# A new order for the steps behind the first sentence's weight transfers

## The chip, the cores and the metric

The kernel runs on one core of a Trainium2 chip. The metric is the device time of one execution in microseconds (us), taken as the median of several runs; lower is better.

## The reference

Eight sentences of 576 tokens go through causal sliding-window attention (window 64, 8 heads of 64), and each sentence then goes whole to one of eight experts, which is picked from the mean of its attention output.

```python
scores = np.where(mask, scale * np.matmul(q, k.transpose(0, 1, 3, 2)), -1e9)   # mask: 0 <= i - j < 64
attn = np.exp(scores - scores.max(-1)); attn /= attn.sum(-1) + 1e-09
x = np.matmul(attn, v)                       # then heads side by side: (8, 576, 512)
logits = x.mean(axis=1) @ w_gate             # (8 sentences, 8 experts)
e_idx, gate_w = argmax(logits), softmax(logits)[e_idx]
out[b] = gate_w[b] * (np.maximum(x[b] @ w1[e_idx[b]], 0) @ w2[e_idx[b]])   # F = 1024
```

## The kernel before

Nothing loops over the work in the usual sense. The table `OPS` at the top of the file lists 890 steps; one loop walks it and calls a small function for each step, with the scheduler set to keep the order as written. So the place of a step in the table is the place of its instructions in the queue of each engine that it uses. An engine takes its instructions strictly in this order; between engines there are only semaphores.

A step is a letter, sometimes letters for an engine or a buffer (`a` ACT, `d` DVE, `m` the shared PSUM pool, `b` a mask added by TensorE), and a number. Units are counted through: unit 5b+i is head pair i of sentence b for i below 4 (512 tokens), and the last 64 tokens of all heads for i = 4.

- Transfers, all on GpSimd's queue: `Q` loads q or k of a sentence (512 KB), `t` the q and k of its last 64 tokens (two transfers of 64 KB, L133), `L` a fifth of its v (128 KB, the last one 64 KB; L141, L145), `W` a half of w1 or w2 of its expert (512 KB; L423, L426; `W4b` and `W4b+1` are w1, `W4b+2` and `W4b+3` are w2), `O` a store of 128 tokens by GpSimd (`o` by SP). `P` reads the picked expert into a register of GpSimd.
- Attention: `T` transposes q and k on TensorE (L225), `U` and `k` copy them out of PSUM, `S` makes scores (L275), `E` the exponential on ACT (L288), `K` the mask product on DVE (L297), `l` the row sums on TensorE (L309), `n` and `R` the logarithm and the reciprocal on ACT (L351, L357), `A` the product with v (L331), `X` the division on DVE (L364). `V` copies v of a sentence once more on DVE, moved by 64 rows (L150, L151); `A` of a sentence needs it.
- Gate of a sentence: `g`, `j`, `G`, `H`, `I`.
- Expert: each `c` is the next chunk of matmuls, for each sentence nine of w1 (L461, the ninth L470) and then nine of w2 (four blocks in two halves of 8 matmuls, L503; the second half is the first to read the second half of w2; then L512). Each `r` empties the PSUM buffer of the oldest finished chunk, on ACT or on DVE (L446, L448, L482, L487).

The chunks share a pool of three PSUM buffers with those `T`, `S` and `A` that carry an `m`; a chunk waits until the buffer used three allocations earlier has been emptied. GpSimd's transfers go round eight semaphores (named DMASW0 to DMASW7 below): a transfer is issued when the one eight places before it has landed.

```python
c, x = op[0], op[1:].lstrip("abdm")
e = op[1:len(op) - len(x)]
if c == "c":
    todo.pop(0)()
elif c in "oO":
    store(nc.sync if c == "o" else nc.gpsimd)
elif c == "r":
    evac.pop(0)(e)
```

Of the kernel before, what the change touches and what calls it, by code (L numbers as in the profile page):

```python
# [1 line left out]
OPS = (  # L2
    "Y0.24 Q0.48 Q1.48 Q0.2 Cd0.24 y i Q1.2 Y1.24 Q3 Cd1.24 z Tm3 Tm2 mb T0 Tm1 ka3 ka2 ka0 "
    "t0 Ud3 Ud2 Q2 Sb3 L0 L3 ka1 L1 L2 E3 Smb2 L4 Ud0 l3 Ud1 t1 S0 T4 E2 kd4 Ud4 n3 Smb1 E0 "
    "Mb K0 E1 R3 Q4 L9 Tm5 Sb4 Tm7 Tm8 Ud5 Q5 ka5 kd8 E4 L5 kd7 l1 n1 T6 l4 n4 Ud7 l2 Sb5 ka6 "
    "n2 R1 R4 l0 V0 A3 Ud6 L7 Am1 n0 E5 T9 X3 Am2 Ud9 S7 R2 L8 E7 Ud8 X1 R0 l5 X2 L6 n5 Smb6 "
    "A0 Am4 K7 ka9 E6 t2 X4 X0 Sb8 l7 g0 n7 T12 j0 Q6 Sm9 Tm10 G0 Ud12 kd12 E8 Ud10 H0 E9 "
    "Tm13 Tm11 R7 K9 l6 R5 ka10 Sb12 Ud11 ka13 V1 n6 Q7 l8 P0 Ud13 W0 I0 kd11 T14 Am5 A7 X7 "
    "A6 Ud14 kd14 L12 n8 X5 E12 R6 l12 n12 Sm14 X6 S11 l9 E14 Smb10 Tm17 E11 n9 T18 W1 Ud17 "
    "A9 W2 E10 S13 kd18 Ud18 L13 Tm15 Ud15 l10 Am8 R8 W3 kd15 ka17 T16 K14 L11 c X8 L14 n10 "  # L10
    "E13 R9 c ra X9 c R10 c rd c g1 K11 rd S17 j1 G1 ra ra c H1 L10 c rd l14 K13 c t3 ra c P1 "
    "n14 Q8 ra c c rd c V2 Ua16 c c ra ka16 l11 A10 X10 Am12 W4 c Q9 R12 X12 n11 ra W5 R11 "
    "A11 rd W6 T19 E17 c l13 n13 R13 Ua19 I1 X11 c Sm18 S15 K17 L15 rd E18 W7 R14 A13 c l17 "
    "ra X13 A14 c L16 L17 X14 g2 n17 Tm20 E15 ra kd19 c Ud20 ra L18 kd20 T22 S19 Sm16 E19 L19 "
    "j2 G2 c P2 t4 K15 E16 Q10 K18 c ra c W8 H2 ra ka22 c ra c c S20 l18 ra rd rd K16 c n18 "
    "Q11 K19 L21 ra Tm21 c c Ua21 Ud22 l16 W9 T23 R17 kd21 L23 V3 c c R18 c ra Am17 Ud23 n16 "
    "ra l15 E20 X17 L22 c R16 ka23 c rd n15 A18 c S23 X18 Sm21 K20 T24 kd24 ra R15 E21 L20 "
    "A16 c l19 L29 ra L24 W10 n19 Ud24 Am15 X16 A19 W11 R19 c X15 l20 E23 n20 L25 I2 c X19 rd "
    "L26 ra Tm26 c g3 K23 kd26 l23 Ud26 R20 c ra Sm22 n23 S24 j3 rd G3 E24 E22 T28 H3 K21 c "
    "Tm27 Ud28 P3 t5 ka27 kd28 l21 L28 rd n21 I3 K24 S26 L27 T25 c V4 W12 c Ua27 ra l24 c K22 "  # L20
    "c ra ra ra Ud25 n24 c R23 Q13 Q12 Am20 X20 R21 c c c rd Am23 W13 kd25 E26 A21 T29 rd X23 "
    "l22 Sm27 W14 W15 n22 E27 S28 V5 c c K26 K27 L32 c R24 l26 c X21 t6 A24 E28 Am22 ra R22 "
    "L30 ra K28 n26 X24 Ud29 kd29 c A27 l27 n27 c X22 ra ra c g4 S25 R26 rd Sm29 j4 G4 L34 "
    "E29 T32 Tm30 kd30 E25 Ud30 c Ua32 H4 K29 P4 ka32 ra c l28 R27 T33 L33 rd Ua33 S30 I4 n28 "
    "c Q15 c ra L31 ra Am26 ka33 c E30 c ra W16 X27 X26 ra l29 c K25 R28 c rd n29 Q14 A28 K30 "
    "c W17 X28 T34 S32 Sm33 ra O O E32 c E33 c K32 l25 n25 R25 c kd34 Am25 A29 W18 c O Ua34 "
    "R29 rd W19 T31 l30 c X29 X25 rd ka31 g5 c c Ud31 O ra K33 rd Sm31 n30 S34 j5 G5 c V6 R30 "
    "P5 rd O E31 H5 c K31 T36 l32 Ud36 rd E34 c t7 c A30 c n32 I5 rd L39 ka36 ra R32 l33 T35 "
    "X30 A32 Ua35 L38 rd c K34 rd c ka35 c n33 T37 ra Sm35 S36 L37 O E35 rd c X32 ra E36 W20 "
    "l34 c L35 n34 c K35 K36 L36 c kd37 R33 c O l31 rd W21 R34 rd c n31 R31 c Ua37 Tm38 O W23 "  # L30
    "Ud38 A33 ra ka38 Am34 l35 T39 X33 c n35 W22 c ra X34 A31 X31 g6 kd39 c O Sm38 R35 O S37 "
    "ra E38 j6 c c G6 P6 Ud39 E37 ra ra c V7 K38 rd H6 c l36 c K37 W24 n36 S39 A35 l37 ra rd "
    "E39 c ra n37 c X35 R36 c A37 c ra l38 Am36 K39 ra c c O R37 rd X37 n38 Am39 X36 O c rd c "
    "I6 l39 W27 R38 c n39 O O A38 rd R39 c W25 W26 ra X39 X38 g7 c j7 O c G7 c ra c P7 rd ra "
    "c c O W29 O c ra c O rd H7 O ra c O c W28 W31 ra O ra O c ra c c ra rd c c c c rd c W30 "
    "I7 O ra O c rd c c ra rd O c O O rd c O rd O O c rd c c O ra c c rd c O rd ra rd c c O "
    "rd O c c ra O O c c c c ra rd o O c ra O c ra o "
).split()

# [554 lines left out]
```

## Time and profile before

| | |
|---|---|
| runs | 204.0, 204.12 and 203.14 us, median 204.0 |
| span of the profiled execution, first to last instruction | 201.9 us |
| what the median has beyond that span | 2.1 us |
| granted TensorE clock | 0.996 |
| TensorE busy, DVE, ACT, GpSimd | 183.5, 119.9, 131.8, 111.0 us |
| moved by DMA | 41.16 MB, mean 204 GB/s |

No time of the profiled execution itself is given beside its span, so the span is what the working below starts from, and 2.1 us are carried over as they are. Rows of the profile have a line of the kernel, an engine, an operation, the tile written and those read; "idle before" is the time in which the engine stood still ahead of an instruction, and what ended it. In the chain of waits each row has start, length and the work.

### The profile page before, as it was taken

What the parts mean: (1) busy time and instruction counts of PE and PEld (TensorE: products, weight loads), DVE (VectorE), ACT (ScalarE), POOL (GpSimd) and SP (SyncE); (2) the same over time, 40 slices, a digit from 0 to 9 for tenths busy, and PEclk for the clock granted to TensorE, in tenths of its full rate; (3) what the DMA queues carried; (4) which work ended last, traced back from release to release, by engine and by line L of the source; (5) the groups of instructions that cost most, each with busy time, mean ns of one, the idle gap of its engine ahead of it and who ended that gap; (6) DMA issues with size and microseconds to landing.
All of it is one profiled execution on the core that took longest, in us unless ns stands there. A gap on an engine that the chain in (4) does not pass through costs nothing.

```text
span 201.9 us, 8105 instructions
## 1 busy us (share of the span) xinstructions
PE 183.5 (91%) x3518; PEld 124.2 (62%) x3522; DVE 119.9 (59%) x347; ACT 131.8 (65%) x247; POOL 111.0 (55%) x158
## 2 busy tenths in 40 slices
PE   0487886899999999999999999999999999999991
PEld 0455564656677756577667666676656666776760
DVE  3527989595477546895877457966494651216410
ACT  2179998876599578977779975757787436321121
POOL 7985939235931593478633552439452716553561
PEclk9999999999999999999999999999999999999998
DMA  6999999999999999999999999999999999999693
GB/s 135 175 188 159 194 162 198 199 198 174 196 201 197 170 198 193 174 201 167 200 206 200 169 195 223 259 208 137 183 237 243 266 254 212 274 212 301 235 325 134
DMA packets 83346, 41.16 MB, mean 204 GB/s; under 512 B 48080, under 2 KB 80976, under 8 KB 83312
## 3 DMA queue, kind: packets, MB, share of 16 engines
q0 software_dynamic: 81936, 39.72, 138.5%
q1 hardware_dynamic: 768, 0.85, 1.3%
q8 instruction: 27, 0.44, 0.8%
q10 hardware_dynamic: 608, 0.08, 0.2%
q14 instruction: 7, 0.06, 0.1%
HBM read 61.88 MB, written 9.44 MB: 353 GB/s over the span
## 4 chain that ended last, share of the span: by engine, by line
PE 77%; DMA 9%; POOL 7%; issue 3%; DVE 2%; ACT 1%; POOLq 0%; DVEq 0%; ACTq 0%
PE ph L461 28%; PE po L503 25%; DMA vw<-in_v_dram 9%; PE tp L225 5%; PE ph L470 4%; PE s L275 4%; PE av L331 3%; PE po L512 3%; PE lb L309 3%; POOL vw L141 2%; POOL km L110 2%; POOL qm L110 1%; POOL out_dram L492 1%; PE gps L392 1%; POOL qkt L133 1%
## 5 line engine op out<-in xcount | busy, mean ns | idle before, releaser
L503 PE MATMUL po<-w2b,hm 128*64 128x512 f16 x512 | 60.1, 379 | 0.0
L461 PE MATMUL ph<-xm,w1b 128*64 128x512 f16 x512 | 60.0, 379 | 0.0
L461 PEld LDWEIGHTS <-w1b 128*64 128x64 f16 x512 | 31.7, 110 | 18.7 <-issue 0.4
L503 PEld LDWEIGHTS <-hm 128*64 128x64 f16 x512 | 30.1, 110 | 19.3
L141 POOL DMA_DIRECT2D vw<-in_v_dram x32 | 28.9, 910 | 13.3 <-DMA w1b<-in_moe_w_dram 4.3
L446 ACT ACTIVATE hm<-ph,gw 128x512 f16<-128x512 f32 x39 | 26.6, 693 | 13.4 <-PE ph L461 13.3
L492 POOL DMA_DIRECT2D out_dram<-ob x31 | 17.2, 557 | 25.0 <-DMA w1b<-in_moe_w_dram 7.0
L351 ACT ACTIVATE ln<-lb 128x512 f32<-128x512 f32 (+1 forms) x40 | 22.5, 563 | 11.8 <-PE lb L309 8.6
L364 DVE CUSTOM_DVE_ANT_0 xm<-av,rl 128x512 f16<-128x512 f32 x32 | 21.6, 686 | 10.4 <-PE av L331 9.5
L482 ACT COPY ob<-po 128x512 f32<-128x512 f32 x18 | 10.6, 586 | 23.6 <-PE po L503 23.6
L448 DVE TENSOR_SCALAR hm<-ph,gw 128x512 f16<-128x512 f32 x25 | 18.7, 748 | 12.1 <-PE ph L461 11.6
L357 ACT ACTIVATE rl<-ln 128x512 f32<-128x512 f32 (+1 forms) x40 | 23.3, 594 | 1.5 <-DVE pool L364 1.3
L225 PE MATMUL tp<-ident,qm 128*64 128x128 bf16 x256 | 13.8, 232 | 7.4 <-DMA qm<-in_q_dram 6.9
L288 ACT ACTIVATE pe<-s 128x1024 f16<-128x1024 f32 x19 | 19.5, 1028 | 1.4 <-PE s L275 0.7
L297 DVE TENSOR_TENSOR pe<-pe,mask 128x1024 f16<-128x1024 f16 x24 | 16.3, 687 | 3.9 <-ACT pe L288 3.1
L252 ACT COPY kT<-tp 128x512 bf16<-128x512 bf16 x19 | 11.2, 597 | 9.0 <-PE tp L225 8.0
L225 PEld LDWEIGHTS <-qm 128*64 128x64 bf16 x256 | 10.7, 118 | 10.0 <-DMA qm<-in_q_dram 6.9
L482 DVE COPY ob<-po 128x512 f32<-128x512 f32 x14 | 9.7, 690 | 10.7 <-PE po L503 10.5
L423 POOL DMA_DIRECT2D w1b<-in_moe_w_dram x16 | 12.6, 785 | 5.9 <-DMA vw<-in_v_dram 2.9
L275 PEld LDWEIGHTS <-kT 64*128 64x128 bf16 x576 | 10.1, 95 | 8.9 <-issue 5.6
L331 PEld LDWEIGHTS <-vw 128*64 128x64 f16 x512 | 12.4, 112 | 4.7 <-issue 1.2
L225 PE MATMUL tp<-ident,km 128*64 128x128 bf16 x256 | 13.9, 231 | 1.4 <-DMA km<-in_k_dram 0.9
(80 smaller groups left out, 267.2 us busy)
## 6 DMA issues: line engine op xcount, KB each, us to landing
w1b<-in_moe_w_dram POOLq DMA_DIRECT2D x16, 512.0 KB, 9.3
w2b<-in_moe_w_dram POOLq DMA_DIRECT2D x16, 512.0 KB, 13.4
out_dram<-ob POOLq DMA_DIRECT2D x31, 256.0 KB, 8.1
vw<-in_v_dram POOLq DMA_DIRECT2D x32, 128.0 KB, 9.0
km<-in_k_dram POOLq DMA_DIRECT2D x7, 512.0 KB, 9.3
qm<-in_q_dram POOLq DMA_DIRECT2D x7, 512.0 KB, 9.0
out_dram<-obt POOLq DMA_DIRECT2D x14, 64.0 KB, 7.7
qkt<-in_q_dram POOLq DMA_DIRECT2D x8, 64.0 KB, 7.6
```

The lines of the kernel that those rows point to most:

```text
L141: nc.gpsimd.dma_start(out=vt[:, 2 * J + 1], in_=v[b, :, 128 * J:128 * J + 128].rearrange("h c d -> c h d"))
L225: nc.tensor.transpose(tp[p0:p0 + 64, n, r], t[:, 2 * i + hh, ts(r, 64)], ident)
L288: nc.scalar.activation(out=po, in_=sp[0], func=AF.Exp, scale=scale)
L351: nc.scalar.activation(out=ln, in_=lb[:, 0:n], func=AF.Ln)
L357: nc.scalar.activation(out=rl, in_=lns.pop((b, i)), func=AF.Exp, scale=-1.0)
L364: nc.vector.tensor_tensor_reduce(out=xm[:, i], in0=av.rearrange("q r p -> q (r p)"), in1=rl, scale=1.0, scalar=0.0, op0=ALU.mult, op1=ALU.add,
L446: nc.scalar.activation(out=o, in_=i, func=AF.Relu, scale=g)
L448: nc.vector.tensor_scalar(out=o, in0=i, scalar1=g, scalar2=0.0, op0=ALU.mult, op1=ALU.max)
L461: nc.tensor.matmul(out=ph[64 * c:64 * c + 64], lhsT=w1t[:, kb, ts(2 * ft + c, 64)], rhs=xm[:, kb], start=(kb == 0), stop=(kb == 3), skip_g ...
L482: copy(e)(out=ob, in_=po)
L492: (nc.scalar if n and eng is nc.sync else eng).dma_start(out=dst, in_=src)
L503: nc.tensor.matmul(out=po[64 * c:64 * c + 64], lhsT=hm[:, fb, ts(2 * r + c, 64)], rhs=w2t[:, fb], start=(fb == 0), stop=(fb == 7), skip_gr ...
```

## The change

The first 197 steps of `OPS` stay, to the fourth w1 chunk of sentence 0. The other 693 stand in a new order. Steps and their number are the same but for the letters: six of the `r` and a few copies change between ACT and DVE (ACT has 6 instructions fewer, DVE 6 more), some `T` and `A` change their PSUM pool, and three stores instead of two are issued by SP. Since the table is one line shorter, line numbers are lower by one. One line of the table, before and after:

```diff
-    "E13 R9 c ra X9 c R10 c rd c g1 K11 rd S17 j1 G1 ra ra c H1 L10 c rd l14 K13 c t3 ra c P1 "
-    "n14 Q8 ra c c rd c V2 Ua16 c c ra ka16 l11 A10 X10 Am12 W4 c Q9 R12 X12 n11 ra W5 R11 "
+    "ra g1 K11 t4 L10 K13 rd S17 c c ra j1 G1 Q9 t3 P1 W4 ra c rd H1 R12 c c rd I1 rd ra c V2 c "
+    "l14 c rd n14 c A12 c l11 c X12 A11 R14 E17 n11 Am10 ka16 rd X10 c l13 c Q8 ra R11 Ua16 "
...
```

First place, GpSimd's queue just behind the unchanged part. `vw2` is v of sentence 2 (`L13` and `L11`, `L14`, then `L10`), `qkt` the last 64 tokens of a sentence, `w1b1` the w1 of sentence 1. Before:

```order
L141 DMA vw2_93<-in_v_dram 128x8x64 [waits DMASW0_49]
L145 DMA vw2_93<-in_v_dram 64x8x64 [waits DMASW1_49]
L141 DMA vw2_93<-in_v_dram 128x8x64 [waits DMASW2_49]
L133 DMA qkt_1237<-in_q_dram 64x8x64 [waits DMASW3_49,PE_49]
L133 DMA qkt_1237<-in_k_dram 64x8x64 [waits DMASW4_49]
L413 TENSOR_LOAD eidx_1194 [waits DVE_49]
L110 DMA qm_1309<-in_q_dram 128x8x256 [waits DMASW5_49,PE_49]
L423 ISA
L423 DMA w1b1_97<-in_moe_w1_dram 128x4x512 [waits DMASW6_49]
```

And now:

```order
L140 DMA vw2_93<-in_v_dram 128x8x64 [waits DMASW0_49]
L144 DMA vw2_93<-in_v_dram 64x8x64 [waits DMASW1_49]
L132 DMA qkt_1163<-in_q_dram 64x8x64 [waits DMASW2_49,PE_49]
L132 DMA qkt_1163<-in_k_dram 64x8x64 [waits DMASW3_49]
L140 DMA vw2_93<-in_v_dram 128x8x64 [waits DMASW4_49]
L109 DMA km_1214<-in_k_dram 128x8x256 [waits DMASW5_49,PE_49]
L132 DMA qkt_1216<-in_q_dram 64x8x64 [waits DMASW6_49,PE_49]
L132 DMA qkt_1216<-in_k_dram 64x8x64 [waits DMASW7_49]
L412 TENSOR_LOAD eidx_1209 [waits DVE_49]
L422 ISA
L422 DMA w1b1_97<-in_moe_w1_dram 128x4x512 [waits DMASW0_49]
```

The two transfers of `t4` now stand ahead of `L10`, the last piece of sentence 2's v that `V2` needs; `L10` has moved from lane 2 to lane 4.

Second place, the same queue a little on, up to the second half of sentence 1's w2 (the second `w2b1`); `vw0` is v of sentence 3. Before:

```order
L423 DMA w1b1_97<-in_moe_w1_dram 128x4x512 [waits DMASW0_49]
L426 ISA
L426 DMA w2b1_100<-in_moe_w2_dram 128x4x512 [waits DMASW1_49]
L141 DMA vw0_91<-in_v_dram 128x8x64 [waits DMASW2_49,DVE_49,PE_49]
L426 ISA
L426 DMA w2b1_100<-in_moe_w2_dram 128x4x512 [waits DMASW3_49]
L141 DMA vw0_91<-in_v_dram 128x8x64 [waits DMASW4_49,PE_49]
```

And now:

```order
L422 DMA w1b1_97<-in_moe_w1_dram 128x4x512 [waits DMASW2_49]
L140 DMA vw0_91<-in_v_dram 128x8x64 [waits DMASW3_49,DVE_49,PE_49]
L140 DMA vw0_91<-in_v_dram 128x8x64 [waits DMASW4_49,PE_49]
L425 ISA
L425 DMA w2b1_100<-in_moe_w2_dram 128x4x512 [waits DMASW5_49]
L140 DMA vw0_91<-in_v_dram 128x8x64 [waits DMASW6_49,PE_49]
L425 ISA
L425 DMA w2b1_100<-in_moe_w2_dram 128x4x512 [waits DMASW7_49]
```

Three pieces of sentence 3's v, not one, now stand ahead of that half of w2.

Third place, DVE around `V2`, the two copies of `vw2`. Before:

```order
L448 TENSOR_SCALAR hm_1104<-ph_1201,gw_829 128x512
L297 TENSOR_TENSOR pe_1119<-pe_1119,mask_111 128x1024
L448 TENSOR_SCALAR ht_1105<-ph_1241,gw_829 128x512
L150 COPY vw2_93<-vw2_93 64x4x512
L151 COPY vw2_93<-vw2_93 64x4x512
L364 ISA xm_1366,pool_1368<-av_1369,rl_1146 128x512
```

And now:

```order
L447 TENSOR_SCALAR hm_1104<-ph_1222,gw_829 128x512
L437 RECIPROCAL gw_1312<-gsum_1233 128x1
L447 TENSOR_SCALAR hm_1104<-ph_1237,gw_829 128x512
L149 COPY vw2_93<-vw2_93 64x4x512
L150 COPY vw2_93<-vw2_93 64x4x512
L481 COPY ob_1347<-po_1316 128x512
L363 ISA xm_1359,pool_1361<-av_1362,rl_1235 128x512
```

Behind `V2` stands now the emptying of the first w2 chunk of sentence 0 (`ob`), and the first `A` of sentence 2 that waits for `V2` is `A12`, not `A10`. On TensorE that first `A` has moved ahead of a w2 half chunk of 8 matmuls and of the two matmuls of `l11`, which stood before it.

65 rows, old and new, of the table OPS are left out of this document.

## The prediction

> **What bounds the kernel now.** I read the page first, then the busy time by stretches, TensorE's waits, and the chain of waits. The page has TensorE busy for 91% of the span, and the DMA engines busy for nine tenths or more of nearly every slice.
>
> ```profile
> span 201.9 us, 8105 instructions
> PE 183.5 (91%) x3518; PEld 124.2 (62%) x3522; DVE 119.9 (59%) x347; ACT 131.8 (65%) x247; POOL 111.0 (55%) x158
> DMA  6999999999999999999999999999999999999693
> GB/s 135 175 188 159 194 162 198 199 198 174 196 201 197 170 198 193 174 201 167 200 206 200 169 195 223 259 208 137 183 237 243 266 254 212 274 212 301 235 325 134
> w2b<-in_moe_w_dram POOLq DMA_DIRECT2D x16, 512.0 KB, 13.4
> vw<-in_v_dram POOLq DMA_DIRECT2D x32, 128.0 KB, 9.0
> ```
>
> Where TensorE's idle time lies tells what a new order can save. By stretches of 10 us (columns: length, then busy us of PE, PEld, DVE, ACT, POOL, clock, DMA, GB/s):
>
> ```profile
> 30.00:40.00 10.00, 7.38 (x223) 5.61 (x221) 7.14 (x19) 8.86 (x17) 6.46 (x8) 1.00 1.48 198
> 40.00:50.00 10.00, 10.00 (x194) 6.20 (x190) 7.24 (x26) 6.76 (x13) 4.59 (x6) 1.00 1.64 189
> 60.00:70.00 10.00, 10.00 (x205) 7.02 (x199) 6.01 (x23) 8.07 (x16) 2.97 (x5) 1.00 1.68 186
> 190.00:200.00 10.00, 7.61 (x80) 5.18 (x74) 1.31 (x2) 2.13 (x4) 5.42 (x11) 1.00 0.80 276
> ```
>
> From 40 us to 190 us TensorE is busy without a break. Its waits are all in the unchanged first part; asked for 41 to 198 us, the same view has no row. The three largest of the whole span:
>
> ```profile
> PE tp L225 <- DMA qm<-in_q_dram: 6.9, 1, 6.9
> PE av L331 <- DVE pool L364: 1.1, 1, 1.1
> PE lb L309 <- ACT ln L351: 1.1, 2, 0.6
> ```
>
> A busy TensorE need not be a fast one, so I look at its rate in the chain of waits (start, length, work):
>
> ```profile
> 41.01 4.32 PE ph L461 x40
> 54.66 0.86 PE po L503 x8
> 56.86 0.22 PE lb L309 x2
> 68.66 0.34 PE s L275 x16
> 94.66 2.59 PE po L503 x24
> 98.78 2.71 PE po L503 x24
> 110.33 1.85 PE ph L461 x16
> 130.66 1.05 PE ph L461 x8
> 166.21 6.90 PE ph L461 x64
> ```
>
> Toward the end, at 166.21, 64 matmuls run with no attention work between them, 0.108 us each. The 40 at 41.01 take the same 0.108, and so do the 8 at 54.66, in the thick of the mixed part. So the changed part runs at TensorE's own rate, and only pieces like those at 98.78, 110.33 and 130.66 are longer than their kind (by 0.12, 0.12 and 0.19). I count eight such in the chain, about 1.0 us together. Several follow an `S`, and both orders enter a run of `S` from other work 15 times, so these will return.
>
> The last rows of the timeline bound the end: TensorE ends at 197.61, and the stores and the closing take the 4.3 us to 201.9.
>
> ```profile
> 196.54 1.07 PE L512 MATMUL po<-w2b,ht 128*64 128x256 f16 x16
> 198.05 0.56 ACTq L492 DMA_DIRECT2D out_dram<-obt  x1
> ```
>
> **The change part by part.** The steps are the same, so TensorE's work behind the fourth chunk is the same. A new order moves the end in two ways: it adds waits on TensorE, each of which goes to the end in full, since nothing later on TensorE is idle and could take it up, or it removes what is longer than its kind.
>
> *Waits that go.* With no listed wait, at most the 1.0 us above. I take -0.2, with bounds -0.8 and 0.
>
> *The first `A` of sentence 2* must wait for `V2`, and `V2` for `L10`. Before, on GpSimd, DVE and TensorE (start, length, idle before):
>
> ```profile
> 40.09 0.88 POOL L141 DMA_DIRECT2D vw<-in_v_dram  x1 [2.27 <-DMA w1b<-in_moe_w_dram]
> 43.09 0.68 POOL L133 DMA_DIRECT2D qkt<-in_k_dram  x1 [1.44 <-DMA w1b<-in_moe_w_dram]
> 51.04 0.69 DVE L150 COPY vw<-vw 64x2048 f16<-64x2048 f16 x1 [0.63 <-DMA qkt<-in_q_dram]
> 51.76 0.76 DVE L151 COPY vw<-vw 64x2048 f16<-64x2048 f16 x1
> 53.98 0.67 PE L331 MATMUL av<-pe,vw 128*64 128x64 f16 x32
> L150 DVE COPY vw<-vw x8: 687/688/959, 20.3 to 148.7; 64x2048 f16<-64x2048 f16 x8
> L151 DVE COPY vw<-vw x8: 689/762/941, 21.3 to 149.4; 64x2048 f16<-64x2048 f16 x8
> ```
>
> DVE waited for a landing and started `V2` at 51.04; by the queue's order this was `L10`, issued at 40.09. `V2` ended at 52.52, and TensorE came to `A10` at 53.98: 1.46 us to spare. Now TensorE gets there earlier by a half chunk (0.86) and a pair (0.22): 0.38 is left. And `t4`, 2 x 64 KB = 0.131 MB, stands ahead of `L10`; at the 189 GB/s of that stretch it takes 0.69 us. `A12` is late by 0.31. A higher bound comes from the lanes: `L10` now has the lane on which a transfer was issued at 43.09, and with the 9.0 us to landing of its kind it lands at 52.1, 1.05 later than before, so 0.67 late. With both copies at their longest (0.959 and 0.941 for 0.69 and 0.76) this becomes 1.1. The lower bound is 0, if the small transfers share the engines with `L10` rather than precede it; a gain is excluded, because TensorE did not wait here. I take 0.5, between the two ways of reckoning. What stands behind the waiting `V2` on DVE is the emptying of w2 chunk 0, and its buffer is asked for again only two half chunks (1.7 us) after `A12`, so it costs nothing more.
>
> *The second half of sentence 1's w2* (`W7`). Before:
>
> ```profile
> 69.95 0.76 POOL L423 DMA_DIRECT2D w1b<-in_moe_w_dram  x1 [2.49 <-DMA vw<-in_v_dram]
> 70.63 1.89 PE L503 MATMUL po<-w2b,hm 128*64 128x512 f16 x16
> ```
>
> The transfer issued at 69.95 is `W8`, eight places behind `W7` and on its lane, so `W7` had landed at about 69.9; TensorE reads it in its second half chunk, at 70.63 + 0.86 = 71.5: 1.6 to spare. Now `t4`, `L16` and `L17` stand ahead of it too: 128 + 256 KB = 0.393 MB, at 186 to 196 GB/s about 2.1 us. TensorE comes earlier, because `S20` (0.34) has moved behind, and later by the 0.5 of `A12`. Late by 2.1 + 0.34 - 1.6 - 0.5 = 0.34. With the bandwidth of the slow slices (159 and 162 GB/s) the 2.1 becomes 2.5, and the whole lateness here 1.2 before `A12`'s part is taken off. Lower bound 0: 13 us and more of queue lie between issue and landing, and one landing can shift by more than 1.2. Since a wait at `A12` gives this transfer time, the two don't add freely: together they are the larger of 0.8 and `A12`'s own, with bounds 0 and 1.2.
>
> *Other transfers.* I went through the weights and q, k in both queues in the same way. Each was in time before, and with the bytes that now stand ahead each keeps a microsecond or more; from the third sentence on the difference between the orders is under 2.5 us and falls where more was to spare. I put nothing for them.
>
> *Emptying the shared PSUM buffers.* At sentence 1's third chunk, TensorE needs the buffer that the `r` of its first chunk empties on ACT, behind `E15`:
>
> ```profile
> 59.83 0.37 ACT L487 COPY obt<-po 128x256 f32<-128x256 f32 x1
> 60.58 1.03 ACT L288 ACTIVATE pe<-s 128x1024 f16<-128x1024 f32 x1
> 61.48 0.70 ACT L446 ACTIVATE hm<-ph,gw 128x512 f16<-128x512 f32 x1
> ```
>
> Before, that buffer was free at 62.18. The copy at 59.83 and one logarithm, which stood ahead of `E15`, have moved away, 0.75 us from 59.83 to 60.58, so it is free at 61.43; TensorE, its steps added up from 43.4 us on at the lengths of their kinds, asks for it at about 61.7 (62.2 behind a wait at `A12`). That is 0.3 to spare where a row of ACT lasts up to 1.03. I found several places with as little. I take 0.1 in all, bounds 0 and 0.6.
>
> *The end.* The store of the last full block goes from GpSimd to SP; its bytes and the copy ahead of it are the same. I take 0, bounds -0.2 and 0.3.
>
> Sum: -0.2 + 0.8 + 0.1 + 0 = +0.7. The span becomes 202.6, and with the same 2.1 us around it the time is 204.7 us.
>
> **The rivals.** *TensorE hides it all.* If `L10` and `W7` land as before or earlier, and nothing waits for ACT, the order does nothing: 204.0 us. For it speaks that no wait stands on TensorE now; against it the two sums, both of which come out late.
>
> *The queue of transfers becomes the bound at sentence 1.* This is the slower side. The place is `W7`; it decides from 1.6 us of added queue on. At the slow slices' bandwidth TensorE loses 1.2 there, and every 128 KB more of delay ahead of it costs another 0.7 to 0.8: 1.9 us with one, 205.9 us. For it speaks that the DMA row shows nines throughout, so nothing ahead of `W7` can be made up. Against it: `W7`'s 1.6 us was measured in a single execution.
>
> *ACT's queue becomes the bound.* If ACT falls 0.3 us behind at places like `E15`, each costs some 0.3; with two of them on top of the sum, 205.3 us.
>
> *TensorE has room.* If what is longer than its kind in the chain goes, all 1.0 us of it, and the loads are in time, the time is 203.0 us. [...]
>
> **How the numbers follow.** Chances: the forecast, 204.3 to 205.0, 0.35; TensorE hides it all 0.22; the queue of transfers 0.26; ACT's queue 0.11; room on TensorE 0.06. Half a per cent, 1.0 us, is about what a measurement of this kernel can tell from no change. Faster by more: 0.06, the last rival. Within it: the first two, 0.57 less 0.01 at the edge = 0.56. Slower by more: 0.26 + 0.11 and that edge = 0.38. The likeliest case's own range is 203.8 to 205.2; for 8 in 10 it must reach into the slower side to 206.2, past the queue rival's 205.9, and down to 203.5, which keeps part of the room rival and the -0.8 bound.
>
> **What would show it.** Right: TensorE's waits gain one row at `A12`, with DVE's second `V2` copy as releaser, of 0.3 to 1.1 us, and one of w2 for `W7`, and TensorE ends at about 198.3. If neither stands there, and its end is at 197.6, the first rival holds. Rows of TensorE waiting for ACT in the sum of 0.5 us or more speak for ACT's queue. A wait for a weight transfer after sentence 1 would show the reckoning of the other transfers wrong. An end of TensorE before 197 us would show the room.

## The result and the profile after

The changed kernel took 215.5 us (median of four runs, 212.49 to 217.78) against 203.71 us before (203.14 to 204.12); the forecast of 204.7 us and its range of 203.5 to 206.2 were wrong. The ratio, 1.0483 (95% interval 1.0422 to 1.0545), compares the two faster runs of the changed kernel, 212.49 and 214.57 us, with before, while the profiled execution, of which the account below is, was one of the two slower ones. It took 216.44 us, with a span of 214.8 us; TensorE ends at 211.18 us instead of 197.61.

The top of the page and its clock row:

```profile
span 214.8 us, 8100 instructions
PE 188.6 (88%) x3522; PEld 122.9 (57%) x3522; DVE 124.8 (58%) x353; ACT 127.6 (59%) x241; POOL 110.8 (52%) x157
...
PEclk9999999999999979999999999999799999999999
...
GB/s 133 175 182 166 186 172 202 201 188 177 198 191 195 142 194 193 193 118 76 182 189 184 190 200 206 224 205 289 185 202 56 151 220 314 195 200 258 314 282 136
```

Two slices of the clock have a dent, and the GB/s row has holes (118 and 76, then 56) that were not there before. TensorE's waits from 41 to 212 us, a view that was empty for before (us in all, times, longest):

```profile
PE po L502 <- issue: 5.6, 3, 2.6
PE po L502 <- DMA w2b<-in_moe_w_dram: 1.6, 1, 1.6
PE ph L469 <- ACT hm L445: 1.1, 1, 1.1
PE av L330 <- DVE vw L150: 0.6, 1, 0.6
PE s L274 <- ACT pe L287: 0.4, 1, 0.4
```

Only the row of `A12`, `av` waiting for `vw`, was forecast with its place. The largest has no releaser: "issue" is time in which the engine waited for nothing that the profile shows. In the timeline its three places are these:

```profile
74.21 1.40 PE L502 MATMUL po<-w2b,hm 128*64 128x512 f16 x7 [2.08 <-issue]
...
127.08 1.27 PE L502 MATMUL po<-w2b,hm 128*64 128x512 f16 x10 [0.91 <-issue]
...
149.09 1.26 PE L502 MATMUL po<-w2b,hm 128*64 128x512 f16 x8 [2.61 <-issue]
```

Counted in the trace from 0, weight loads, matmuls and the few records of semaphores together, the instructions at which TensorE stands are number 2497, 4545 and 5313 in its queue. All three are 193 modulo 256. At each of them one transfer of the instruction queue lies in or at the edge of the gap (window 71.7 to 72.9 us of the DMA view; the two others alike at 124.7 and 146.8):

```profile
q0 software_dynamic: 1245, 0.16, 206.4%
q8 instruction: 1, 0.02, 5.0%
```

It carries 16 KB (the 27 transfers of this queue on the page are 0.44 MB), and TensorE goes on 1.33 to 1.41 us after its end. The three are the ninth, the 17th and the 20th of these 27, and 9, 17 and 20 times 256, plus 193, are the numbers above. So I call the multiples of 256 in this count block ends, and the k-th transfer the block that goes with the end at 256 k; that a block begins to arrive so much behind the end of the one in use means the time from instruction 256 k to the start of transfer k. My reading, theory 1 below, is that TensorE runs out of instructions: it has 193 behind a block's end, and the next are not there. The other blocks agree: in all 13 profiles of this case, behind 41 us, TensorE passed that place no sooner than 1.2 us after the end of the block's transfer (1.30 us in after, at 101.0 us, and 1.37 in before, at 108.1).

The clock behind these standstills, in windows (length, busy PE, PEld, DVE, ACT, POOL, clock, DMA, GB/s):

```profile
70.00:80.00 10.00, 7.92 (x133) 5.36 (x129) 5.12 (x9) 3.38 (x7) 8.60 (x11) 0.83 1.58 167
...
76.00:78.00 2.00, 2.00 (x13) 1.06 (x11) 1.41 (x3) 0.00 (x0) 1.84 (x3) 0.50 1.28 191
...
150.00:160.00 10.00, 9.64 (x150) 5.68 (x148) 4.70 (x19) 5.07 (x10) 2.63 (x4) 0.84 1.15 197
```

Behind the two long standstills the granted clock falls to half for 3.4 us (74.7 to 78.1 and 149.8 to 153.2 by the trace's clock records), and 13 matmuls take the 2 us in which, at 0.108 us each, 18 run. TensorE had been idle for 2.08 and 2.61 us there; behind the second standstill, with 0.91 us, the records stay at full. But a standstill as long as these two does not always do it: in a run below (a_fix), 2.88 us of idle TensorE ahead of 147.7 us left the clock at full:

```profile
147.00:149.00 2.00, 1.34 (x14) 0.73 (x16) 0.68 (x1) 0.00 (x0) 1.67 (x3) 1.00 1.36 373
```

The account of TensorE's 13.57 us, each gap from the start of the last matmul to that of the next, less the usual distance of such steps:

| place | cause | us |
|---|---|---|
| 53.1 | `A12` waits for `V2` | 0.78 |
| 71.7, 125.8, 146.1 | no instructions | 2.34 + 1.07 + 2.80 |
| behind the first and third | clock at half | 1.59 + 1.85 |
| 95.9 | the ninth w1 chunk of sentence 2 waits for ACT to empty its PSUM buffer | 1.27 |
| 186.4 | the second half of sentence 6's w2 (`W27`) | 1.76 |
| | sum | 13.46 |

The stores give back a little: the span ends 3.7 us behind TensorE instead of 4.3.

### The profile page after: what moved, and what is told of

Its sections match the earlier page's. It is cut to its first block, busy times and chain, and to the rows that moved or that the text cites. A ratio compares the mean times of both kernels' runs of the same rounds, so it can differ in the third digit from the quotient of the medians.

```text
span 214.8 us, 8100 instructions
## 1 busy us (share of the span) xinstructions
PE 188.6 (88%) x3522; PEld 122.9 (57%) x3522; DVE 124.8 (58%) x353; ACT 127.6 (59%) x241; POOL 110.8 (52%) x157
## 4 chain that ended last, share of the span: by engine, by line
PE 63%; DMA 16%; ACT 10%; issue 5%; DVE 3%; POOL 1%; POOLq 0%; DVEq 0%; ACTq 0%
PE po L502 24%; PE ph L460 18%; DMA w1b<-in_moe_w_dram 5%; DMA vw<-in_v_dram 4%; PE tp L224 4%; DMA w2b<-in_moe_w_dram 4%; PE s L274 3%; PE po L511 3%; DMA km<-in_k_dram 3%; PE ph L469 3%; PE av L330 3%; PE lb L308 2%; ACT ln L350 2%; ACT pe L287 2%; ACT rl L356 2%
## 5 line engine op out<-in xcount | busy, mean ns | idle before, releaser
L502 PE MATMUL po<-w2b,hm 128*64 128x512 f16 x512 | 64.2, 395 | 7.2 <-issue 5.6
L460 PE MATMUL ph<-xm,w1b 128*64 128x512 f16 x512 | 60.7, 380 | 0.1
L460 PEld LDWEIGHTS <-w1b 128*64 128x64 f16 x512 | 28.8, 110 | 19.9 <-issue 0.5
L140 POOL DMA_DIRECT2D vw<-in_v_dram x32 | 29.2, 921 | 12.9 <-DMA w1b<-in_moe_w_dram 2.9
L445 ACT ACTIVATE hm<-ph,gw 128x512 f16<-128x512 f32 x36 | 24.8, 688 | 16.2 <-PE ph L460 16.0
L481 DVE COPY ob<-po 128x512 f32<-128x512 f32 x19 | 13.1, 690 | 28.3 <-PE po L502 28.1
L447 DVE TENSOR_SCALAR hm<-ph,gw 128x512 f16<-128x512 f32 x28 | 20.4, 746 | 4.6 <-PE ph L460 4.0
L144 POOL DMA_DIRECT2D vw<-in_v_dram x8 | 5.5, 693 | 22.6 <-DVE hm L447 16.1
L481 ACT COPY ob<-po 128x512 f32<-128x512 f32 x13 | 7.7, 589 | 15.6 <-PE po L502 15.4
L425 POOL DMA_DIRECT2D w2b<-in_moe_w_dram x16 | 12.6, 789 | 6.7 <-PE po L502 2.2
L330 PE MATMUL av<-pe,vw 128*64 128x64 f16 x512 | 13.8, 197 | 1.8 <-DVE pool L363 1.1
```

What stands on the lines that cost most here:

```text
L140: nc.gpsimd.dma_start(out=vt[:, 2 * J + 1], in_=v[b, :, 128 * J:128 * J + 128].rearrange("h c d -> c h d"))
L330: nc.tensor.matmul(out=av[p0:p0 + 64, :, 16 * m:16 * m + 16], lhsT=vt[:, m, 2 * i + hh], rhs=pe[:, hh, m], start=(m == 0), stop=(m == 7), ...
L445: nc.scalar.activation(out=o, in_=i, func=AF.Relu, scale=g)
L447: nc.vector.tensor_scalar(out=o, in0=i, scalar1=g, scalar2=0.0, op0=ALU.mult, op1=ALU.max)
L460: nc.tensor.matmul(out=ph[64 * c:64 * c + 64], lhsT=w1t[:, kb, ts(2 * ft + c, 64)], rhs=xm[:, kb], start=(kb == 0), stop=(kb == 3), skip_g ...
L481: copy(e)(out=ob, in_=po)
```

## The experiments

Theory 1: TensorE's instruction supply makes the standstills, so they depend on where its dense stretches lie against the block ends (1a: the block comes late because transfers fill the DMA engines; 1b: it comes at a pace of its own). Theory 2: the moved transfers and copies make the loss. Theory 3 came later: single pieces are slower in the new order.

**Moving the block ends.** A few small matmuls with their weight loads at the very start, where TensorE waits for its first data, move every block's end against the work and leave the order of all steps as it was.

```diff
 OPS = (
-    "Y0.24 Q0.48 ...
+    "F112 Y0.24 Q0.48 ...
...
-                    nc.tensor.matmul(out=wps, lhsT=warm[:, 0:128], rhs=warm, start=True, stop=True)
+                    nc.tensor.matmul(out=wps[p0:p0 + 64, 0:64], lhsT=warm[:, 0:64], rhs=warm[:, 0:64], ...)
```

Each of these matmuls has its weight load: `F112` adds 224 instructions (a224), `F32` adds 64 (a64, b64), `F128` adds 256 (b256).

On the new order:

> The changed kernel with 224 more TensorE instructions (112 small weight loads and matmuls on a zero tile, read by nobody) ahead of its first transpose, where TensorE waits for q anyway; all steps keep their order. Theory 1, TensorE runs out of instructions: in the changed kernel TensorE stood still, without a releaser, three times, each at an instruction whose number is 193 above a multiple of 256, while a 16 KB block of instructions (256 of them) was still being fetched; 224 more instructions put the block ends elsewhere, where 193 instructions take 3.4 us or more, not 2.5 to 3.3. The three stand-stills go or shrink to under 1 us in sum, and with them the slow clock behind them: 204 to 208 us. Theory 2, the new order itself makes TensorE wait for data (the w2 halves, the emptying of PSUM): the waits stay at the same matmuls and the time at 212 to 218 us.

> The changed kernel with 64 more TensorE instructions (32 pairs) at the start. Theory 1: the block ends fall where 193 instructions take only 1.7, 2.0 and 2.7 us (near 137, 93 and 117 us of the undisturbed time): stand-stills of 1 to 4 us there, at other matmuls than in the changed kernel, again at numbers 193 above a multiple of 256; 212 to 222 us. Theory 2: the same waits at the same matmuls as in the changed kernel.

And on the old one:

> The kernel before with 64 more TensorE instructions (32 pairs) at the start. Theory 1: the old order is as sensitive; its block ends now fall where 193 instructions take 1.6, 2.3 and 2.4 us (near 136, 156 and 79 us): stand-stills of 1 to 4 us each without a releaser, 207 to 216 us. Theory 2: no change, 203.2 to 204.5 us.

> The kernel before with 256 more TensorE instructions (128 pairs) at the start, one whole block: a control of what the added work itself costs. Both theories: the block ends stay where they were, 203.2 to 205 us and no stand-still behind 41 us.

| kernel | median (range), us | ratio to before, 95% | standstills at 189 |
|---|---|---|---|
| a224 | 209.97 (209.25 to 212.16) | 1.0292, 1.0245 to 1.034 | 0.81 and 2.23 |
| a64 | 212.8 (211.63 to 214.47) | 1.0424, 1.0362 to 1.0486 | 1.34, 1.52 and 3.09 |
| b64 | 208.19 (207.71 to 208.59) | 1.0218, 1.0173 to 1.0263 | 0.96, 0.54 and 1.30 |
| b256 | 204.12 (203.49 to 205.23) | 1.0027, 0.9999 to 1.0055 | none |

(In the profiles of these four the place counts as 189, since four matmul records are missing near the start. The standstills are those behind the first w1 chunk, as the whole distance between two starts; by this measure after has 2.46, 1.29 and 2.99.) The waits of a64 and of b64 on "issue":

```profile
PE av L330 <- issue: 4.2, 2, 2.9
...
PE ph L460 <- issue: 1.0, 1, 1.0
```

```profile
PE s L275 <- issue: 1.1, 1, 1.1
PE ph L461 <- issue: 0.6, 1, 0.6
PE al L339 <- issue: 0.3, 1, 0.3
```

The standstills stayed at the same place in the block and, in a64 and b64, moved to other lines. With 64 instructions in idle time the old order loses 4.6 us too, 2.8 of them on TensorE behind its first w1 chunk; with 256, which leaves the block ends where they were, it loses nothing. This is theory 1, and it says something about the old time: 204 us belongs to the order together with its place against the block ends.

The places were forecast less well. a224 was to have under 1 us of standstills, and 204 to 208 us; it kept 3.0 and took 210. Of the six places named ahead for a64 and b64 three had a standstill over 0.5 us, and three came where none was named (near 44 us in both, and 121 us in b64). A short time for 193 instructions made a place a candidate and no more: in after the shortest such time was 2.95 us, from 98.08 us on, and TensorE did not stand there; the block had begun to arrive 0.27 us behind the end of the one in use.

**Undoing the named waits.** `t4` goes behind `L10`, one copy of `T25` from ACT to DVE, `W27` right behind `W26`:

```diff
-    "ra g1 K11 t4 L10 K13 rd S17 c c ra j1 G1 Q9 t3 P1 W4 ...
+    "ra g1 K11 L10 K13 rd S17 c c ra j1 G1 Q9 t3 t4 P1 W4 ...
-    "c c ra ra g3 j3 Tm25 R23 Ua25 E24 ...
+    "c c ra ra g3 j3 Tm25 R23 Ud25 E24 ...
-    "O W24 W26 ra c ...
+    "O W24 W26 W27 ra c ...
```

> The changed kernel with three moves and one letter undone, TensorE's instructions and their order untouched: t4 back behind L10, the q copy of T25 on DVE like its k copy, and W27 up to just behind W26. Expected at the three places that these are for: the wait of A12 for V2 (0.8 us in the changed kernel), the wait of sentence 2's ninth w1 chunk for the copies of T25 (1.3 us), the wait for W27 (1.8 us) go to under 0.3 us each. Theory 1 (instructions run out): the stand-stills at numbers 193 above a multiple of 256 stay, one or more of them over 1 us, so the time is 207 to 213 us, still far above the kernel before. Theory 2 (the waits for data of the new order explain it): with them gone the time is within 1 us of the kernel before.

Measured: 213.63 us (213.12 to 214.66), ratio 1.0487 (1.0441 to 1.0533). Waits from 41 us on:

```profile
PE po L502 <- issue: 5.8, 3, 2.9
PE po L502 <- DMA w2b<-in_moe_w_dram: 1.8, 1, 1.8
PE ph L469 <- ACT hm L445: 0.6, 1, 0.6
...
```

The row of `A12` is gone, that of the ninth w1 chunk is 0.6 instead of 1.1, `W27` is in time, but now the w2 half of sentence 7 (`W31`) is late by 1.8. The three standstills stay (2.19, 1.43 and 3.26 from start to start), and the ratio is the same as that of after. Theory 2 falls as an account of the whole; its waits are real and small.

**Taking transfers away.** Without most of the weight transfers (sentences 3 to 7 then use the weights of sentences 0 to 2), 1a and 1b should part:

```diff
+        if b >= 3:
+            return
         s = WSLOT[b]
```

> The changed kernel without the weight transfers of sentences 3 to 7, which then compute with the weights of sentences 0 to 2; TensorE's instructions are the same. 20 of the 32 weight halves, 10 MB, leave the queue, all from about 90 us on. Theory 1a, a block of instructions comes late because it queues behind the data transfers: the blocks come in less than 5 us from there on, and the stand-stills near 126 and 146 us go, while that near 72 us stays; 206 to 210 us. Theory 1b, the blocks come at a pace of their own, 256 instructions in about 6 us whatever else is moved: the stand-stills near 126 and 146 us stay.

Measured: 207.53 us (206.69 and 208.37), ratio 1.0178 (1.0117 to 1.024). The standstill near 146 is gone, that near 125 stays at 1.42, as neither theory had it. The one at 72, ahead of which nothing was changed, is missing as well: its block began to arrive 0.85 us behind the end of the block in use, instead of 3.28. A small one, 0.54, is new at 99.1. In after, a block begins to arrive between 1.6 us before and 3.7 us behind the end of the one in use, and here the same steps have a standstill at 72 us in one execution and none in another.

What the DMA engines move ahead of a block says more. Here are the stretches ahead of the block that TensorE lacked at 125 us (118.6 to 122.5 us), and ahead of one that came behind it (129 to 133 us):

```profile
DMA packets 1221, 0.76 MB, mean 196 GB/s; under 512 B 219, under 2 KB 1158, under 8 KB 1221
...
DMA packets 0, 0.00 MB, mean 0 GB/s; under 512 B 0, under 2 KB 0, under 8 KB 0
```

The first of these blocks began to arrive 3.06 us behind the end of the one in use, against 3.13 for the same block in after; the second 1.06 us ahead of it, against 1.65 behind in after. Five blocks of this run have almost nothing moving in the 4 us ahead of them (1 GB/s at most), and they came 0.4 to 2.7 us ahead; in after the same five came between 0.3 ahead and 2.0 behind. So the standstill at 125 is no sign against 1a, since data was still being moved there. This speaks for 1a and against a pace of the block's own, in one profile. The amount moved is not the whole of it: with 311 GB/s ahead of it one block came 2.7 us ahead.

**Fewer instructions in the dense stretches.** The ninth w1 chunk is 128 instructions in 1.0 us, the densest there are. With 128 columns to a weight load it is 64 for the same product:

```diff
-                    for c in range(2):
-                        nc.tensor.matmul(out=ph8[64 * c:64 * c + 64, f],
-                                         lhsT=w1t[:, kb, ts(2 * f + c, 64)], rhs=xt[:, kb], ...)
+                    nc.tensor.matmul(out=ph8[:, f], lhsT=w1t[:, kb, ts(f, 128)], rhs=xt[:, kb], ...)
```

> The changed kernel with the ninth w1 chunk of each sentence in 32 matmuls with a stationary side of 128 columns instead of 64 with 64 columns: the same result with 64 pairs less on TensorE, 128 instructions less, no, 64 less, in the place where they stand densest. Theory 1: the stand-stills behind the ninth chunks (near 72, 126 and 146 us) shrink to under 1 us in sum. What the chunk itself then takes is open: 0.9 to 2.6 us against 1.0, so the time is 203 to 218 us, and the verdict is in the stand-stills. Theory 2: the waits stay.

> The same wider ninth chunk in the kernel before, as a control: it has no stand-still to lose, so the time moves only by what the eight chunks take more or less, -1 to +13 us, and by the block ends that move with 64 instructions less a sentence: where 193 instructions behind a block end then take under 3 us, a stand-still appears.

On the new order: 209.01 us (207.0 to 209.74), ratio 1.0218 (1.0152 to 1.0284); of the standstills one of 1.02 is left. On the old order: 204.24 us (203.92 to 204.95), ratio 1.0025 (1.0008 to 1.0043): there the edit has nothing to gain, and a chunk takes 1.04 us instead of 1.01. The edit also moves the block ends, by 64 instructions a sentence, so it does not show by itself that thinning out the stretch removed the standstills.

**Both together.** To the wide chunk and the three edits above come the last sentence's weights:

```diff
-    "g7 O ... H7 ra P7 O W28 W29 O O O c O W30 c c c c W31 O rd ...
+    "g7 O ... H7 ra P7 W28 W29 W30 W31 O O O O c O c c c c O rd ...      # a_all
+    "g7 O ... H7 ra P7 O W28 W29 O O O c O W30 W31 c c c c O rd ...      # a_end
```

> The new order with the ninth chunk of w1 written as 32 matmuls with 128 columns (as in a_c1t), t4 issued behind L10, Ud25 in place of Ua25, W27 issued right behind W26, and W28 to W31 issued right behind P7, ahead of the stores. Theory 1 with the transfers as the rest: a_c1t had 0.91 (A12), 1.17 (T25), 1.02 (standstill near 144) and 2.65 (W27) of gaps; three of these are undone by the edits (T25 in part, a_fix left 0.6 more than nothing), so 209.0 less about 4.2 = 204.8 us, no wait of po for w2b over 0.5, and at most one standstill of about 1. Theory 3 (the new order is slower in pieces too, which the gaps don't show): 206.5 or more, with the gaps gone. If a wait for a weight remains behind 170 us, the transfers of sentences 6 and 7 are late for P6, not for the stores: 206 to 207 with the row naming W24 or W27.

> a_all with 160 TensorE instructions more in its idle start, so that every block of 256 ends elsewhere: by the times of a_c1t the shortest use of 193 instructions behind a block's end is 4.1 us there. Theory 1: no standstill over 0.5 us, 0.5 to 1.5 us under a_all, about 203.8. Theory 3: as a_all within 0.4, 206 or more.

> a_all with less of the stores held back: t4 behind L10, Ud25, W27 behind W26, the ninth chunk of w1 with 128 columns, and of the last sentence's weights only W31 moved, four chunks forward, right behind W30; W28 to W30 stay where the new order has them. In a_all TensorE ended 158.7 us after the start of its first w1 chunk behind the unchanged part (before with the wide chunk: 157.7, the new order 170.1), and the span ended 5.9 us behind TensorE (before: 4.3). Theory 1 (standstills and the named waits are the whole loss, the held-back stores the rest of a_all's time): 158.5 to 159.0 again, no row of po for w2b over 0.5 us, 3.6 to 4.5 us from TensorE's end to the span's, so 204.5 to 206. If W31 is late once more, a row of 0.5 to 1.5 for w2b and as much on top. Theory 3 (pieces are slower in the new order): as a_all, 207.8.

Measured: a_all 207.93 us (204.8 to 208.11, too far apart for an interval), a_all160 207.79 (206.28 to 209.32), ratio 1.0214 (1.015 to 1.0279), a_end 206.95 (205.74 to 210.21), ratio 1.0164 (1.0115 to 1.0212). Theory 1 had forecast 204.8 and 203.8 for the first two, which missed by 3 and 4 us; by the times alone these two are the case of theory 3 (206.5 or more with the gaps gone). a_end lies in theory 1's case with `W31` late. The profiles say what the misses are. Since the first data lands at varying times, TensorE's part is taken from its first w1 chunk (40.5 to 41.7 us in these profiles) to its end:

| kernel | from the first w1 chunk to TensorE's end | from there to the span's end |
|---|---|---|
| before | 156.8 | 4.3 |
| after | 170.1 | 3.7 |
| old order, wide chunk (b_c1t) | 157.7 | 4.3 |
| new order, wide chunk (a_c1t) | 163.7 | 3.7 |
| a_all | 158.7 | 5.8 |
| a_all160 | 158.8 | 4.2 |
| a_end | 159.9 | 3.7 |

Waits of a_all, of which its whole list is this, and of a_end:

```profile
PE ph L468 <- ACT hm L445: 0.6, 1, 0.6
PE s L274 <- ACT pe L287: 0.4, 1, 0.4
PE lb L308 <- DVE pe L296: 0.2, 1, 0.2
```

```profile
PE po L500 <- DMA w2b<-in_moe_w_dram: 0.7, 1, 0.7
PE ph L468 <- ACT hm L445: 0.6, 1, 0.6
PE av L330 <- DVE vw L150: 0.4, 1, 0.4
...
```

Behind the first w1 chunk no standstill is left in any of the three profiles (a_all160 has one of 1.0 us just ahead of it, in the unchanged part), and 158.7 is 1.0 above the old order with the same chunk, about the rows that remain. So on TensorE the standstills with the clock behind them and the named waits are the whole loss, and theory 3 has no room beyond a few tenths. The rest of these kernels' time is not TensorE's: in a_all the held-back stores make the end 1.5 us longer, and its first chunk starts 0.9 us later than before's. The runs of each of these versions vary by 3 to 4.5 us (the profile of a_all160 is of its fastest, 206.28 us), and which wait makes that spread was not seen. None of the versions beats the old order.

## Why the prediction was wrong

**The step that failed** is the sentence "A new order moves the end in two ways", with the reading under it that the changed part "runs at TensorE's own rate". The length of a piece is indeed the same in both orders. But the order also sets how many instructions fall behind a block's end, and this third way cost 6.21 us of standstill and 3.44 us of slow clock, 9.65 of 13.46. The trace of before had a sign of it. Its waits from 5 to 46 us, in the unchanged first part, hold this row, which I passed over as small:

```profile
PE tp L225 <- issue: 0.5, 1, 0.5
```

It is at instruction 1213, 189 modulo 256 (this profile lacks the four records too). Behind 41 us the old order had the margin, and no view of waits shows how little: its fastest 193 instructions behind a block's end took 3.09 us (from 67.2 us), and there the next block happened to begin to arrive after 0.45 us. At 63.9, 90.1 and 108.1 us TensorE passed the place only 1.4 to 1.5 us after its block had landed, the delay at which it goes on after a standstill.

**`A12`**, 0.5 with bounds 0 and 1.1, was right in place and kind and came to 0.78:

```profile
52.06 0.84 DVE L149 COPY vw<-vw 64x2048 f16<-64x2048 f16 x1 [2.52 <-DMA vw<-in_v_dram]
52.94 0.94 DVE L150 COPY vw<-vw 64x2048 f16<-64x2048 f16 x1
...
53.93 0.38 PE L330 MATMUL av<-pe,vw 128*64 128x64 f16 x12 [0.59 <-DVE vw L150]
```

`V2` starts 1.02 us later than before. The reckoning by lanes had 1.05, the one by bytes 0.69: the lane came nearer. The copies took 0.34 us longer than before, inside the bound. That 0.78 is nearly the 0.8 which stood in the sum for `A12` and `W7` together is luck: one part came out larger and the other was nothing.

**`W7`**, 0.34, did not happen: it landed at 70.7 us, before the half chunk in front of its first reader had begun (71.43). The rival built on this place, the queue of transfers at sentence 1, did not occur.

**"I put nothing for them"**, on the other transfers, was wrong by 1.76 us. I had taken the difference between the orders as "under 2.5 us" from the third sentence on. For `W27` it is far more, and the table shows it: 103 chunks stand ahead of it in the old order, 118 in the new one, 15 chunks or some 13 us of TensorE, and the very next chunk in the table is its first reader. It was issued at 180.0 us, with 19 store steps ahead of it instead of 12, and landed at 188.3, when TensorE had stood for 1.6 us:

```profile
163.93 0.72 POOL L144 DMA_DIRECT2D vw<-in_v_dram  x1 [10.51 <-DVE hm L447]
...
180.00 0.76 POOL L425 DMA_DIRECT2D w2b<-in_moe_w_dram  x1 [2.10 <-PE gps L391]
...
188.37 1.92 PE L502 MATMUL po<-w2b,hm 128*64 128x512 f16 x16 [1.59 <-DMA w2b<-in_moe_w_dram]
```

The first row shows where the stores were held up: from 153.4 to 163.1 us GpSimd's queue stands at `P6`, which waits for the picked expert of sentence 6 (DVE's row that finds it ends at 163.0), and the next transfer is issued at 163.9, while the DMA engines run empty:

```profile
160.00:170.00 10.00, 10.00 (x172) 5.82 (x170) 8.24 (x20) 6.66 (x14) 6.07 (x10) 1.00 0.47 95
```

I had counted the bytes ahead of each transfer, and not the register reads that close the queue. That `P6` adds to `W27`'s delay is read from the order and these rows; no run moved `P6` alone. That its place in the queue does is shown by a_fix, where it stands behind `W26` and is in time.

**Emptying PSUM**, 0.1 with a bound of 0.6, came to 1.27, at a place I had not worked out, but by the mechanism of the rival on ACT's queue, and with its sign (rows of TensorE waiting for ACT, 1.1 and 0.4):

```profile
95.17 0.57 ACT L241 COPY qt<-tp 128x512 bf16<-128x512 bf16 x1
...
96.64 0.70 ACT L445 ACTIVATE hm<-ph,gw 128x512 f16<-128x512 f32 x1
...
97.38 0.79 PE L469 MATMUL ph<-xt,w1b 128*64 128x64 f16 x39 [1.10 <-ACT hm L445]
```

The ninth w1 chunk of sentence 2 starts 0.04 us after ACT has emptied the buffer of the seventh, and from 94.1 us up to that moment ACT worked without a pause. One of the rows ahead was the q copy of `T25`. With this copy on DVE (a_fix) ACT came to the buffer sooner, and the wait fell to 0.6. It is not the buffer of `T25` itself, for in a_fix that one was still being copied when the chunk was already running:

```profile
95.00 0.79 PE L469 MATMUL ph<-xt,w1b 128*64 128x64 f16 x39 [0.62 <-ACT hm L445]
...
95.41 0.68 DVE L251 COPY kT<-tp 128x512 bf16<-128x512 bf16 x1
```

So here the buffer asked for is the one given out two allocations earlier, not three as the description of the kernel has it.

**Waits that go**, -0.2, can be neither seen nor excluded: the account leaves 0.1 open, and the first w1 chunk started 0.2 us later than before. **The end**, 0 with bounds -0.2 and 0.3, was -0.6, outside its bounds. With the rows that the steps had (0.78, 1.27, 1.76) a full working would have come to some 3.8 us, 207 to 208; only the instruction supply, with the slow clock behind it, takes it to 215.

## What to carry to other kernels

Before an order of small matmuls is trusted, count its TensorE instructions in blocks of 256 and look for dense stretches behind a block's end; a wait on "issue" at the same number modulo 256 is the mark (193 here, with rows of 0.91 to 2.61 us in after). The count gave candidates and not the places: three of six in a64 and b64. Shift the whole queue by a few idle-time instructions and measure again: where the time moves by per cents (2.2 in b64), it belongs to the placement as much as to the order. When a transfer changes places, count the steps of the bounding engine between it and its use, and every register read in its queue that waits for other engines (at `P6` GpSimd's queue stood for 9.7 us).

## What I had not expected of the hardware

In seven kernels TensorE stood still at number 193 (or 189, with four records missing) modulo 256, and went on 1.3 to 1.6 us after the end of the 16 KB transfer that goes with that place; why it is 193 was not shown. In after a block began to arrive from 1.6 us ahead to 3.7 us behind the end of the block in use. In a_noW five blocks came 0.4 to 2.7 us ahead where almost no data was moved; how transfers of data would delay a block stays open. The same 64 instructions, in time that was idle, made the old order 2.2% slower.

In each of the 13 profiles the clock records change only at whole multiples of 3.41 us, counted from the first rise to full clock (in after it rises at 13.28 us, and the changes, at 74.72, 78.13, 149.81, 153.22 and 214.66 us, are 18, 19, 40, 41 and 59 of them later). From 41 us to TensorE's end every such stretch with 2.08 us or more of idle TensorE was followed by half clock (four: two in after, one each in a224 and a64), and none with 1.85 us or less was (ahead of 41 us two with 1.67 and 1.68 were). In a_fix the 2.88 us of idle time were split by such a point into 1.25 and 1.64, and the clock stayed at full.
